# Casting the keys' and channel weights' high parts on GpSimd instead of ScalarE

## Chip, cores and metric

The kernel runs on one core of one Trainium2 chip. The metric is the device time of one execution in microseconds (us); three runs of the kernel before gave 1030.22, 1030.34 and 1031.10 us, with a median of 1030.34 us.

## The reference, cut to what matters

Three parts follow one another. Everything is fp32 at the interface; there are 4 batches, 8 heads, 576 tokens, head dimension 64.

```python
# 1. attention with a threshold, per batch and head
scores = q @ k.T / 8
scores = where(scores >= max(scores) - tau, scores, -1e9)
attn = softmax(scores)
x = (attn @ v)                       # heads side by side: [4, 576, 512]
# 2. token mixing of rank 32, then a channel layer
u = x + (x.T @ U @ V).T
x = u + relu(u @ w_ch1) @ w_ch2      # 512 -> 2048 -> 512
# 3. a mixture of 8 experts, one expert per token
out[token] = p[e] * relu(x[token] @ w1[e]) @ w2[e]
```

## The kernel before, in words

**Numbers in two parts.** TensorE (PE) multiplies in a shortened fp32 form here (`F32R` in the code). To keep the precision, many operands are split: a high part, which is the number rounded to that form, and a low part, which is the number less its high part. A product is then built from two or three matmuls. The splitting costs one copy (the high part) and one subtraction (the low part) for each tile.

**Attention.** The 8 heads of a batch are handled as 4 pairs, so there are 16 pairs `i`, 0 to 15, with batch `b = i // 4`. `load_pair` (L261) loads one pair. It walks over `cuts`: for pairs 1 to 15 these are two cuts of the keys (576 and 640 columns, `kq` = 1) and then two of the queries (608 columns each). Each cut is one DMA from the queue on SyncE (SP) into a raw tile `x` (three such buffers, L281), then the split: for keys the high part `kh` by ScalarE (ACT, L289) and the low part `kl` by the engine called `eng` (L290), which is GpSimd (POOL) for pairs 1 to 7 and VectorE (DVE) for pair 0 and for batches 2 and 3 (L271). For queries ACT makes the high part (L292) and DVE the low one (L294). The tiles `kh` and `kl` have two buffers each, so those of a pair come free when the scores of the pair two before it are done.

Per pair there are five groups of rows, and the scores of a pair come in nine tiles of 576 columns. A tile goes through: scores on PE (L313, L315), row maximum on DVE (L348), exponential on ACT (L359), a limit and then mask with row sum on DVE (L352, L363). There are two PSUM buffers for scores, so the scores of a tile wait for the mask of the tile two before it. The back half transposes the result on PE (L416, L422), copies it to SBUF on ACT (L417, L423, L424), multiplies by the values (L435 to L439), and then a chain of small steps (`chain`, L447) does the token mixing.

**Stages.** Batch 0 has attention alone (`attention_alone`, L553): while its tiles run, ACT and DVE also convert the channel weights from their 64-bit form (`narrow`, L198; a cast on ACT at L212, a join on DVE at L219), which SP writes to DRAM (`wdram`). `turn_over` (L580) puts dummy matmuls into PE's gaps. Then batches 1 to 3 run their attention interleaved with the channel layer of the batch before (`channel`, L725). The channel layer takes its weights from `wdram` with `load_w` (L664): one tile for each of the two layers per block `f` (16 blocks), each split into `hi` and `lo`. In batch 0 the high part is made by ACT for `f` 0 and 1 and by POOL after that (L677 to L680); the low part is by POOL in batch 0 (L676, L681). After the last attention come the last channel layer, the routing, and the experts.

**What sets the order.** The instructions are written in program order with data dependences; a planner places them on the engines' queues by its own estimates of their times, earliest first where inputs and buffers are ready. Each engine then works through its queue in order. Only in `attention_alone` is the order of one engine, POOL, kept as written (L855). So moving an instruction to another engine can also move others on all queues.

The choice of engine for the high part in `load_w`:

```python
eng = dve if b and (b < B - 1 or f < 8) else pool
if b == 0 and f > 1:
    pool.tensor_copy(hi, x)
else:
    act.activation(hi, x, AF.Copy)
```

Of the kernel before, what the change touches and what calls it, by code (L numbers as in the profile page):

```python
# [14 lines left out]
AF = mybir.ActivationFunctionType  # L15
# [88 lines left out]
def attention_channel_moe(ctx, tc, qk, vv, tau, umat, vrep, wch, wgl, wexp, consts, out):  # L104
    nc = tc.nc
    pe, dve, act, pool, sp = nc.tensor, nc.vector, nc.scalar, nc.gpsimd, nc.sync
# [146 lines left out]
    def scalars():  # L253

        sp.dma_start(out=t8[:, 0:1], in_=tau)

        dve.tensor_scalar(out=t8[:, 1:2], in0=t8[:, 0:1], scalar1=NEGTAU, scalar2=0.125, op0=ALU.is_ge, op1=ALU.mult)
        dve.tensor_scalar(out=t8[:, 2:3], in0=t8[:, 1:2], scalar1=0.0, scalar2=BIG, op0=ALU.is_equal, op1=ALU.mult)
        dve.tensor_scalar(out=t8[:, 0:1], in0=t8[:, 0:1], scalar1=0.0, scalar2=t8[:, 2:3], op0=ALU.max, op1=ALU.add)

    def load_pair(b, hp, later=None):  # L261

        i = b * NPAIR + hp
        v = ap.tile([128, VW], F32, tag="v", name=f"v{i}")
        qs = ap.tile([128, QKW], F32R, tag="qs", name=f"qs{i}")
        kh = ap.tile([128, QKW], F32R, tag="kh", name=f"kh{i}")
        kl = ap.tile([128, QKW], F32R, tag="kl", name=f"kl{i}")

        cuts = ((0, 0, 128), (1, 0, S), (0, 704, 832), (1, S, QKW), (0, 128, 704), (0, 832, QKW)) if i == 0 else (
            (1, 0, S), (1, S, QKW), (0, 0, 608), (0, 608, QKW))  # L270
        eng = dve if i == 0 or b > 1 else pool  # L271
        def steps():
            for n, (kq, c0, c1) in enumerate(cuts):
                c = slice(c0, c1)
                nm = f"raw{i}_{n}"
                if (i, n) == (0, 1):
                    x = mlp.tile([128, S], F32, tag="yr", name=nm, bufs=2)
                elif i == 0 and c1 - c0 == 128:
                    x = mlp.tile([128, 512], F32, tag="wr", name=nm, bufs=WR)
                else:  # L280
                    x = ap.tile([128, 640], F32, tag="raw", name=nm, bufs=3)  # L281
                x = x[:, :c1 - c0]
                sp.dma_start(out=x, in_=qk[i][:, kq, c])
                if (i, n) == (0, 0):
                    scalars()
                if (i, n) == (0, 3):
                    sp.dma_start(out=cst, in_=consts)
                if kq:
                    act.activation(kh[:, c], x, AF.Copy)  # L289
                    eng.tensor_tensor(out=kl[:, c], in0=x, in1=kh[:, c].bitcast(F32), op=ALU.subtract)  # L290
                else:
                    act.activation(qs[:, c], x, AF.Copy, scale=t8[:, 1:2])  # L292
                    lo, hi, xl = qs[64:128, c], qs[64:128, c].bitcast(F32), x[64:128]
                    dve.scalar_tensor_tensor(out=lo, in0=xl, scalar=t8[64:128, 1:2], in1=hi,  # L294
                                             op0=ALU.mult, op1=ALU.subtract)
                yield
            sp.dma_start(out=v, in_=vv[i])

        if later is None:
            for _ in steps():  # L300
                pass
        else:
            later.append(steps())
        return qs, kh, kl, v
# [359 lines left out]
    def load_w(b, f):  # L664
        nm = f"{b}_{f}"
        if f >= NF or nm in W:
            return
        while DONE[0] < f:
            next(conv, None)
        r = []  # L670
        for i, bufs in ((0, W0), (1, W1)):
            x = mlp.tile([128, 512], F32, tag="wr", name=f"wr{nm}_{i}", bufs=WR)
            sp.dma_start(out=x, in_=wdram[f * 128:f * 128 + 128, i * 512:i * 512 + 512])
            hi = mlp.tile([128, 512], F32R, tag=f"w{i}h", name=f"w{i}h{nm}", bufs=bufs)
            lo = mlp.tile([128, 512], F32R, tag=f"w{i}l", name=f"w{i}l{nm}", bufs=bufs)
            eng = dve if b and (b < B - 1 or f < 8) else pool  # L676
            if b == 0 and f > 1:  # L677
                pool.tensor_copy(hi, x)
            else:
                act.activation(hi, x, AF.Copy)  # L680
            x = eng.tensor_tensor(out=lo, in0=x, in1=hi.bitcast(F32), op=ALU.subtract)  # L681
            if i == 0:
                LAST[:] = [x.ins]
            r.append((hi, lo))
        W[nm] = r
# [39 lines left out]
    def channel(p):  # L725
        hs = {}
        load_w(p, 0)
        load_w(p, 1)
        for f in range(NF):
            yield from mlp_l1(p, f, hs)  # L730
            if f % 4 == 0 and f:
                yield from mlp_l2(p, f - 4, hs)
            load_w(p, f + 2)
        HS[p] = hs
# [640 lines left out]
```

## Time and profile before

| What | Value |
|---|---|
| median of three runs | 1030.34 us |
| the profiled execution, its own time | 1029.61 us |
| its span, first to last instruction | 1027.8 us |
| mean granted TensorE clock | 0.996 of full speed |
| PE busy, share of the span | 995.2 us, 97% |
| DVE busy | 719.3 us, 70% |
| ACT busy | 611.8 us, 60% |
| POOL busy | 152.2 us, 15% |

The profiled execution's own time has 1.8 us that lie around its span. A row of the trace gives an engine and an operation with the source line, "out<-in" names, shapes, a count, busy time and a mean; behind a bar or in brackets stands how long the engine sat idle just before it and what ended that. Busy shares are averages over stages that have different limits, so the stretches of the span are read one by one.

### The profile page before, as it was taken

What the parts mean: (1) busy time and instruction counts of PE and PEld (TensorE: products, weight loads), DVE (VectorE), ACT (ScalarE), POOL (GpSimd) and SP (SyncE); (2) the same over time, 40 slices, a digit from 0 to 9 for tenths busy, and PEclk for the clock granted to TensorE, in tenths of its full rate; (3) what the DMA queues carried; (4) which work ended last, traced back from release to release, by engine and by line L of the source; (5) the groups of instructions that cost most, each with busy time, mean ns of one, the idle gap of its engine ahead of it and who ended that gap; (6) DMA issues with size and microseconds to landing.
All of it is one profiled execution on the core that took longest, in us unless ns stands there. A gap on an engine that the chain in (4) does not pass through costs nothing. (4 is left out here: it accounts for less than half of the span.)

```text
span 1027.8 us, 17859 instructions
## 1 busy us (share of the span) xinstructions
PE 995.2 (97%) x6352; PEld 836.2 (81%) x6352; DVE 719.3 (70%) x1761; ACT 611.8 (60%) x1242; POOL 152.2 (15%) x143
## 2 busy tenths in 40 slices
PE   7898999989999999999999999999999999999996
PEld 4666677768787787788889898999998998889984
DVE  7998697776778877877676664683369755566673
ACT  6888777776677777776565653422354444455562
POOL 1332245342000000000000000013400321120100
PEclk9999999999999999999999999999999999999998
DMA  6655577864323322423121110453055555566550
GB/s 213 220 153 162 160 257 245 273 209 140 116 92 94 125 72 83 127 90 94 55 68 42 42 43 31 139 207 122 25 192 180 177 202 185 174 192 198 196 184 16
DMA packets 58241, 143.72 MB, mean 140 GB/s; under 512 B 7389, under 2 KB 8157, under 8 KB 58144
## 3 DMA queue, kind: packets, MB, share of 16 engines
q1 hardware_dynamic: 54784, 132.27, 40.0%
q0 software_dynamic: 3360, 10.23, 3.1%
q8 instruction: 52, 0.85, 0.3%
q14 instruction: 45, 0.37, 0.1%
HBM read 124.65 MB, written 18.61 MB: 139 GB/s over the span
## 5 line engine op out<-in xcount | busy, mean ns | idle before, releaser
L1125 ACT ACTIVATE eh<-ew 128x512 fp32r<-128x512 f32 x160 | 94.2, 628 | 68.1 <-PE el L1241 47.7
L1126 DVE TENSOR_TENSOR el<-ew,eh 128x512 fp32r<-128x512 f32 x160 | 106.7, 692 | 37.7 <-ACT eh L1125 36.2
L702 PE MATMUL l<-uh,w0h 128*128 128x256 f32 (+2 forms) x352 | 127.0, 361 | 0.3 <-ACT yT L508 0.3
L363 DVE SCALAR_TENSOR_TENSOR p<-s,st,p 128x576 f32<-128x576 f32 x144 | 114.1, 814 | 15.8 <-ACT p L359 12.4
L359 ACT ACTIVATE p<-s,st 128x576 f32<-128x576 f32 x144 | 103.7, 738 | 33.1 <-DVE st L348 31.6
L703 PE MATMUL l<-ul,w0h 128*128 128x256 f32 (+2 forms) x352 | 122.6, 348 | 0.0
L704 PE MATMUL l<-uh,w0l 128*128 128x256 f32 (+2 forms) x352 | 122.3, 348 | 0.0
L348 DVE TENSOR_REDUCE st<-s 128x1 f32<-128x576 f32 x144 | 105.1, 749 | 18.0 <-PE s L315 17.4
L717 PE MATMUL l<-hh,w1h 128*128 128x512 f32 (+3 forms) x320 | 115.2, 360 | 0.0
L719 PE MATMUL l<-hh,w1l 128*128 128x512 f32 (+3 forms) x320 | 112.8, 353 | 0.0
L718 PE MATMUL l<-hl,w1h 128*128 128x512 f32 (+3 forms) x320 | 112.2, 351 | 0.0
L417 ACT ACTIVATE ptt<-tp 128x512 f32<-128x512 f32 (+1 forms) x192 | 88.4, 490 | 30.1 <-PE tp L416 30.0
L313 PE MATMUL s<-kh,qs 128*128 128x288 f32 x320 | 95.5, 318 | 5.6 <-DVE p L363 3.6
L681 POOL TENSOR_TENSOR w1l<-wr,w1h 128x512 fp32r<-128x512 f32 x24 | 31.7, 1333 | 457.5 <-DVE rha L984 426.6
L416 PE MATMUL tp<-cst,p 128*128 128x128 f32 x576 | 90.8, 276 | 5.2 <-ACT ptt L417 5.0
L722 DVE TENSOR_TENSOR yT<-l,yT 128x448 f32<-128x448 f32 (+2 forms) x96 | 50.0, 521 | 57.9 <-PE l L719 57.5
L315 PE MATMUL s<-kl,qs 128*128 128x288 f32 x320 | 88.5, 296 | 0.0
L373 ACT ACTIVATE p<-p,rv 128x576 f32<-128x576 f32 x108 | 78.6, 771 | 15.3 <-DVE rv L380 15.0
L416 PEld LDWEIGHTS tp<-cst,p 128*128 128x128 f32 x576 | 67.8, 140 | 20.6 <-ACT ptt L417 11.4
L313 PEld LDWEIGHTS s<-kh,qs 128*128 128x128 f32 x320 | 60.3, 188 | 15.6 <-DVE p L363 6.4
L435 PE MATMUL po<-ptt,v 128*64 128x256 f32 (+1 forms) x256 | 69.8, 413 | 2.4 <-ACT ptt L424 1.5
L706 DVE SCALAR_TENSOR_TENSOR hl<-l,hh 128x512 fp32r<-128x512 f32 (+2 forms) x80 | 46.3, 578 | 36.7 <-ACT hh L705 36.4
(604 smaller groups left out, 2468.6 us busy)
## 6 DMA issues: line engine op xcount, KB each, us to landing
ew<-in_wexp_dram SPq DMA_DIRECT2D x80, 512.0 KB, 4.6
wr<-wdram SPq DMA_DIRECT2D x128, 256.0 KB, 3.1
cr<-in_wch_dram SPq DMA_DIRECT2D x32, 512.0 KB, 5.2
raw<-in_qk_dram SPq DMA_DIRECT2D x30, 304.0 KB, 3.2
wdram<-w SPq DMA_DIRECT2D x32, 256.0 KB, 3.0
v<-in_vv_dram SPq DMA_DIRECT2D x16, 352.0 KB, 3.9
raw<-in_qk_dram SPq DMA_DIRECT2D x16, 320.0 KB, 3.8
raw<-in_qk_dram SPq DMA_DIRECT2D x17, 288.0 KB, 3.0
```

The lines of the kernel that those rows point to most:

```text
L313: pe.matmul(s["t"][:, h, :288], lhsT=qs[:, qc:qc + 128], rhs=kh[:, k0:k0 + 288], start=(j == 0), stop=False)
L348: dve.tensor_reduce(out=self.st[:, 0, h:h + 1], in_=self.t[h], axis=AX.XY, op=ALU.max, negate=True)
L359: act.activation(self.halves(h), self.t[h], AF.Exp, bias=self.st[:, 0, h:h + 1])
L363: dve.scalar_tensor_tensor(out=p, in0=self.t[h], scalar=self.st[:, 1, h:h + 1], in1=p, op0=ALU.is_ge, op1=ALU.mult, accum_out=self.rvs[:, ...
L416: pe.transpose(tp[:, c - c0], src[:, c * 128:c * 128 + 128], ident)
L702: pe.matmul(pm, lhsT=w1h[:, wk], rhs=uh[k], start=(k == 0), stop=False)
L703: pe.matmul(pm, lhsT=w1h[:, wk], rhs=ul[k], start=False, stop=False)
L704: pe.matmul(pm, lhsT=w1l[:, wk], rhs=uh[k], start=False, stop=(k == 3))
L717: pe.matmul(pm, lhsT=w2h[:, wd], rhs=xh, start=(f == f0), stop=False)
L718: pe.matmul(pm, lhsT=w2h[:, wd], rhs=xl, start=False, stop=False)
L719: pe.matmul(pm, lhsT=w2l[:, wd], rhs=xh, start=False, stop=(f == f0 + 3))
L1126: dve.tensor_tensor(out=lo, in0=x, in1=hi.bitcast(F32), op=ALU.subtract)
```

## The change

It does two things. In `load_pair`, where the low parts of the keys are already POOL's (pairs 1 to 7), POOL also makes the high parts with a copy. In `load_w`, POOL makes the high parts of all blocks of batch 0, those of `f` 0 and 1 too.

```diff
@@ load_pair
                 if kq:
-                    act.activation(kh[:, c], x, AF.Copy)
+                    if eng is pool:
+                        pool.tensor_copy(kh[:, c], x)
+                    else:
+                        act.activation(kh[:, c], x, AF.Copy)
                     eng.tensor_tensor(out=kl[:, c], in0=x, in1=kh[:, c].bitcast(F32), op=ALU.subtract)
@@ load_w
             eng = dve if b and (b < B - 1 or f < 8) else pool
-            if b == 0 and f > 1:
+            if b == 0:
                 pool.tensor_copy(hi, x)
             else:
                 act.activation(hi, x, AF.Copy)
```

## Rows read from the trace of the kernel before

**Rows 1.** Busy time by stretch: start:end, length, PE, PEld, DVE, ACT, POOL (instructions).

```profile
8.00:103.00 95.00, 81.91 (x568) 59.27 (x567) 87.85 (x207) 76.73 (x159) 25.72 (x20) 1.00 0.61 188
103.00:240.00 137.00, 130.15 (x787) 99.59 (x786) 107.26 (x225) 101.93 (x198) 51.78 (x50) 1.00 0.72 231
240.00:622.00 382.00, 381.29 (x2444) 314.23 (x2443) 271.84 (x678) 256.57 (x520) 7.54 (x8) 1.00 0.26 81
...
750.00:1000.00 250.00, 249.19 (x1500) 223.31 (x1500) 166.50 (x373) 119.23 (x238) 36.59 (x35) 1.00 0.56 186
```

**Rows 2.** Waits of DVE, 8 to 103 us: total us, times, longest.

```profile
DVE st L348 <- PE s L315: 4.6, 7, 1.2
DVE p L363 <- ACT p L359: 1.2, 2, 0.9
DVE qs L294 <- ACT qs L292: 0.4, 1, 0.4
```

**Rows 3.** Waits of PE, 8 to 103 us.

```profile
PE tp L416 <- ACT ptt L417: 5.0, 7, 1.3
PE s L313 <- DVE p L363: 2.8, 4, 2.2
PE s L313 <- DVE st L352: 1.7, 2, 1.5
PE po L435 <- ACT ptt L423: 0.6, 2, 0.3
PE idle L585 <- ACT ptt L417: 0.6, 1, 0.6
```

**Rows 4.** ACT's key copies (L289) by form and waits of ACT, 8 to 103 us.

```profile
L289 ACT ACTIVATE kh<-raw 128x640 fp32r<-128x640 f32 x5 | 3.7, 738 | 0.6 <-DMA raw<-in_qk_dram 0.6
L289 ACT ACTIVATE kh<-raw 128x576 fp32r<-128x576 f32 x5 | 3.4, 681 | 1.4 <-issue 0.8 <-POOL w1l L681 0.6
...
ACT qs L292 <- DMA raw<-in_qk_dram: 2.3, 4, 0.8
```

**Rows 5.** ACT's high parts of weight blocks 0 and 1, from L680, 0 to 103 us.

```profile
L680 ACT ACTIVATE w0h<-wr x2: 632/632/632, 46.3 to 60.4; 128x512 fp32r<-128x512 f32 x2
L680 ACT ACTIVATE w1h<-wr x2: 621/629/637, 50.2 to 68.4; 128x512 fp32r<-128x512 f32 x2
```

**Rows 6.** POOL's work by form, 8 to 103 us.

```profile
L290 POOL TENSOR_TENSOR kl<-raw,kh 128x640 fp32r<-128x640 f32 x5 | 8.3, 1651 | 0.0
L290 POOL TENSOR_TENSOR kl<-raw,kh 128x576 fp32r<-128x576 f32 x5 | 7.5, 1495 | 18.6 <-ACT kh L289 18.5
...
L678 POOL CAST w1h<-wr 128x512 fp32r<-128x512 f32 x1 | 0.6, 612 | 15.9 <-DMA wr<-wdram 15.9
```

**Rows 7.** DVE by form, 8 to 103 us, and the line L219 over the span.

```profile
L294 DVE SCALAR_TENSOR_TENSOR qs<-raw,t,qs 64x608 fp32r<-64x608 f32 x10 | 9.3, 926 | 0.7 <-ACT qs L292 0.4
L219 DVE SCALAR_TENSOR_TENSOR w<-cr,top 128x512 int32<-128x512 int32 x7 | 7.6, 1085 | 0.0
...
L379 DVE TENSOR_SCALAR rv<-rv 128x4 f32<-128x4 f32 x8 | 3.5, 444 | 0.1
...
L219 DVE SCALAR_TENSOR_TENSOR w<-cr,top x32: 670/690/1721, 32.0 to 231.8; 128x512 int32<-128x512 int32 x32
```

**Rows 8.** Order of time, one meeting of DVE and POOL: start, us.

```profile
155.40 1.13 DVE L219 SCALAR_TENSOR_TENSOR w<-cr,top 128x512 int32<-128x512 int32 x1
...
155.38 0.61 POOL L678 CAST w1h<-wr 128x512 fp32r<-128x512 f32 x1 [3.18 <-PE l L718]
```

**Rows 9.** Order of time: pair 2's keys, its first scores; then L313 by stretch.

```profile
31.41 0.69 POOL L237 TENSOR_TENSOR vst<-wv,vst 32x64 fp32r<-32x64 f32 x2 [0.93 <-DVE vst L235]
32.18 3.35 POOL L290 TENSOR_TENSOR kl<-raw,kh 128x576 fp32r<-128x576 f32 x2
...
51.54 0.30 PE L313 MATMUL s<-kh,qs 128*128 128x288 f32 x1
...
0.00:51.53 51.53, 12.91 (x40) 7.68 (x41) 1.00 0.68 216
```

**Rows 10.** Waits of SP's queue, 8 to 103 us; first use of the channel weights.

```profile
SPq L283 <- POOL kl L290: 23.1, 8, 9.4
...
L702 PE MATMUL l<-uh,w0h x352: 277/365/631, 113.3 to 745.2; 128*128 128x512 f32 x64, 128*128 128x256 f32 x48, 128*128 128x448 f32 x32, 128*128 128x320 f32 x32
```

**Rows 11.** Waits of PE, 103 to 240 us.

```profile
PE tx L461 <- ACT yT L442: 2.0, 2, 1.2
PE po L435 <- ACT ptt L424: 1.5, 2, 0.8
```

## The prediction

> **What bounds the kernel now.** I read the busy time by stretch first [rows 1]. From 240 us on PE is busy for 381.29 of 382 us and for 249.19 of 250 us; PE is the bound there and nothing in the change touches that part. In 103 to 240 us (attention of batch 1 beside the channel layer of batch 0) PE still works 130.15 of 137 us. Only 8 to 103 us is different: PE 81.91 of 95 us, dummy matmuls included, DVE 87.85, ACT 76.73, POOL 25.72. So in the first attention DVE is the engine that is nearly full (92%), ACT follows with 81%, and PE waits for both. A shorter first stretch moves everything behind it forward by the same amount, since PE then works without a gap.
>
> Next, what DVE waits for in that stretch [rows 2]: 4.6 us for scores from PE, 1.2 us for an exponential from ACT, 0.4 us for a query cut from ACT. These 6.2 us are nearly all of its 7.15 idle us, and they are the most that the stretch can lose unless DVE gets less work, which the change does not give it. Why scores are late is seen in the waits of PE [rows 3]: the listed waits on ACT come to 6.2 us, those on DVE to 4.5 us. PE takes its queue in order, so scores stand behind a transpose that waits for ACT to empty its PSUM tile. That is the way in which a full ACT reaches DVE.
>
> **Part 1, ACT gets less work.** In 8 to 103 us there are ten key copies (pairs 1 to 5): 5 x 0.738 + 5 x 0.681 = 7.1 us by the two forms [rows 4]. The four weight copies of blocks 0 and 1 are 2 x 0.632 + 2 x 0.629 = 2.5 us [rows 5]. ACT thus loses 9.6 of 76.7 us, and goes from 81% to 71%. It also loses about 2 us in which it stood still in front of a key copy whose DMA or buffer was not ready [rows 4], with exponentials queued behind. What this is worth on the path: at least nothing, at most the 6.2 us of DVE's waits. I take the 1.6 us that ACT itself ended (1.2 + 0.4) in full, and 1.0 us of the 4.6 us that came through PE: ACT has more than half of PE's waits, some 2.7 of the 4.6, and I count a little over a third of that because ACT's load falls by an eighth only and some of the waits are PE's own matmuls at the end of a pair. Gain 2.6 us.
>
> **Part 2, POOL gets more work.** A copy of 128x512 takes POOL 0.612 us [rows 6]. By the number of columns I estimate 0.69 us for 576 and 0.765 us for 640. Fourteen copies in the stretch are 5 x 0.69 + 5 x 0.765 + 4 x 0.612 = 9.7 us; POOL goes from 25.7 to 35.4 of 95 us. POOL itself is not the bound.
>
> But POOL's instructions hold up some of DVE's. A join on DVE that starts 0.02 us after a POOL copy of 0.61 us takes 1.13 us [rows 8]; its usual duration is 0.69 us [rows 7]. So a plain copy does it too, at 0.44 us in this case. What it costs in sum is read from the means of the three kinds that are stretched [rows 7]: joins 7 x (1.085 - 0.69) = 2.8 us; the query cuts 10 x (0.926 - 0.85) = 0.8 us; the small 128x4 additions at 8 x (0.444 - 0.16) = 2.3 us, where 0.85 and 0.16 us are my estimates of what such an instruction takes undisturbed, from the shortest part of each group. That is 5.9 us of DVE's time against 25.7 us of POOL's: 0.23 us per us of POOL work. For 9.7 us this gives 2.2 us. The other end is half of that, 1.1 us: what a collision costs is what is left of POOL's instruction, so the cost per instruction grows with the square of its length, and the copies are half as long as POOL's subtractions (0.7 against 1.3 to 1.65 us). I take the middle, 1.6 us, since the copies stand directly in front of the subtractions and do not come at free moments.
>
> The Trainium skill (SBUF — State Buffer, "Who interferes with whom") states that VectorE with two SBUF inputs and GpSimd reading SBUF share an exclusive port, and that the second to start blocks fully until the first is done. By that alone that join [rows 8] would lose the 0.59 us left of the copy instead of 0.44 us, and the 1.6 us would become about 2.1 us. The row decides, and the sum stays with 1.6 us.
>
> **Part 3, the order of things inside a pair.** POOL now does copy, subtraction, copy, subtraction on its own queue, where ACT's copies ran ahead of it. For pair 2, whose subtractions stand behind POOL's `vst` work until 32.1 us [rows 9], the first subtraction ends 0.7 us later. SP's load of the last query cut waits for that raw buffer [rows 10], and ACT's query copy waits for the load (2.3 us, four times [rows 4]), with exponentials behind it. Bounds: 0.7 us earlier for a pair where POOL was idle and ACT busy, 0.7 us later where POOL is busy; for five pairs -3.5 to +3.5 us. I take nothing: both kinds occur, and the finished keys have much room (pair 2 is done at 35.5 us and first used at 51.54 us: a pair has 20 matmuls of line L313, and 40 lie before that [rows 9]). If the planner puts the query copy too early on ACT, this cover is gone, at up to 0.7 us each.
>
> The four weight copies cost nothing beyond the port: they are made by 70 us and used from 113.3 us on [rows 10]. POOL waits for their DMA as it does for the ones after them, and only low parts that need the same data stand behind.
>
> **Part 4, 103 to 240 us.** The four copies of pairs 6 and 7 leave ACT (2 x 0.738 + 2 x 0.681 = 2.8 us of 101.9) and put 2.9 us on POOL. PE is the bound, with 6.85 us idle; the two longest waits on ACT are 2.0 and 1.5 us [rows 11]. Gain between nothing and 0.5 us, taken as nothing. The port takes 0.7 us from DVE at the same rate, hidden because DVE is busy for 78% only; without that cover it costs 0.7 us.
>
> **Sum.** -2.6 + 1.6 = -1.0 us on the profiled execution of 1029.61 us: 1028.6 us. That execution lies 0.73 us below the median of 1030.34 us, so in terms of the median: **1029.3 us**. About 0.2% (2.1 us) is what a measurement of this kernel can tell from no change; the forecast is inside that.
>
> There is one cost without a row: the planner places all queues anew. The bound for it is PE's idle time that an order can win or lose, 13.1 us in the first stretch and 6.85 us in the second; a fifth of it, 4 us either way, is my estimate.
>
> **Rivals.**
> - *ACT was the hidden bound of the first stretch* (chance 0.34). PE's longest waits are for ACT [rows 3]. If the lighter ACT clears DVE's waits almost wholly and the port costs the low end, it is -6.2 + 1.1 = -5.1 us at most, 1025.2 us; with half of the 6.2 us plus 1 us from the second stretch, -3.0 us, 1027.3 us. Against it: DVE has 92% of the stretch without any help, and its waits on ACT are 1.2 and 0.4 us.
> - *The port makes it slower* (chance 0.23). Where copy and subtraction of one cut follow each other without a pause, POOL is in the way for about 2.2 us instead of 1.5 us, and a join or a query cut that arrives can lose all of it. At one and a half times the rate, 0.34 us per us, 9.7 us cost 3.3 us; if ACT's relief is worth nothing because DVE is the bound, this is +3.3 us: 1033.6 us. It decides from the point where the holding costs 2.1 us more than the relief gives. For it: DVE is the fullest engine and works 20 us of the stretch in instructions that can be held. Against it: at today's rate the cost is at most 2.2 us. The Trainium skill (Perfetto Trace Analysis, "Optimizing Scalar/DVE Operations") warns that moving work between these two engines might not help because of the shared port; no run so far shows it for the move from ACT.
> - *Nothing moves* (part of the 0.43 for "same"). The copies lay in ACT's own idle time, 18 us of the stretch, so relief and port are both small: 1030.3 us.
>
> **How the numbers follow.** The forecast and "nothing moves" lie within 2.1 us of 1030.34 us: 0.43. Faster 0.34, slower 0.23. The range goes from 1025.0 us (first rival at its end) to 1034.5 us (second rival with some of part 3); the forecast's own range is 1028.2 to 1032.4 us.
>
> **What would show it.** In 8 to 103 us ACT should be near 67 us busy, POOL near 35 us, and the joins' mean a little above 1.085 us. DVE's waits on ACT should be nearly gone, the first pair of batch 1 should begin 1 us earlier. POOL copies should measure 0.69 and 0.765 us. Wrong would be: DVE's stretched instructions growing by over 3 us, new waits of ACT for query DMAs, or a first stretch that is shorter with the time given back in 103 to 240 us.

## The result and the profile after

The changed kernel is slower. Eleven runs have a median of 1037.58 us (1033.59 to 1040.54); eleven runs of the kernel before on the same chip have 1030.35 us (1029.36 to 1032.84). The ratio is 1.0066, with a 95% interval of 1.0055 to 1.0077. The forecast was 1029.3 us, and the result lies outside its range (1025.0 to 1034.5 us). The profiled execution after took 1037.8 us, with a span of 1036.0 us; each is 8.2 us more than in the profiled execution before.

Line numbers of the changed kernel are 3 higher from L293 on (POOL's key copy is L290, ACT's is L292); in the kernels of the experiments they are shifted by up to 5 lines. First the busy time by stretch; columns as in [rows 1], where PEld is the weight load of PE and the last three numbers are the granted clock, the DMA share and GB/s.

```profile
8.00:103.00 95.00, 80.74 (x535) 56.86 (x535) 83.65 (x199) 66.44 (x136) 33.76 (x33) 0.96 0.56 176
103.00:240.00 137.00, 127.21 (x752) 95.46 (x751) 107.70 (x217) 98.97 (x191) 58.83 (x56) 1.00 0.68 222
240.00:622.00 382.00, 381.32 (x2455) 314.95 (x2454) 276.62 (x687) 257.10 (x519) 7.56 (x8) 1.00 0.27 86
```

Against [rows 1]: ACT fell by 10.3 us and POOL rose by 8.0 us in the first stretch, as meant. But DVE, which sets that stretch, fell too, by 4.2 us: it was not relieved, it stood still. PE's idle time in the second stretch rose from 6.85 to 9.79 us. From 240 us on PE is as full as before. One row says how the loss is spread: the first and the last use of the channel weights.

```profile
L705 PE MATMUL l<-uh,w0h x352: 276/366/632, 119.2 to 753.9; 128*128 128x512 f32 x64, 128*128 128x256 f32 x48, 128*128 128x448 f32 x32, 128*128 128x320 f32 x32
```

Before it was 113.3 to 745.2 us [rows 10]: 5.9 us are lost before the channel layer of batch 0 begins, 2.8 us after that. The seventeenth row maximum on DVE, at 46.22 us before and 52.39 us after, is already 6.2 us late, so nearly all of the first stretch's loss is made by then.

What DVE, PE and ACT waited for in 8 to 103 us (total, times, longest), from the waits of the changed kernel:

```profile
DVE st L351 <- PE s L318: 7.5, 14, 1.3
PE s L316 <- DVE p L366: 6.0, 5, 2.2
ACT qs L295 <- DMA raw<-in_qk_dram: 2.6, 3, 1.3
PE idle L588 <- ACT ptt L420: 2.2, 1, 2.2
ACT p L362 <- DVE st L351: 10.7, 12, 2.4
DVE qs L297 <- ACT qs L295: 0.7, 1, 0.7
```

and the last but one of these in the kernel before:

```profile
ACT p L359 <- DVE st L348: 3.7, 7, 1.4
```

DVE waits 7.5 us for scores instead of 4.6 us, 14 times instead of 7 [rows 2]. PE's longest wait of before, for ACT to empty a transpose (5.0 us [rows 3]), is down to 0.3 us, but PE now waits 6.0 us for masks of DVE instead of 2.8 us, and ACT 10.7 us for row maxima instead of 3.7 us: ACT is lighter, and stands longer. ACT's waits for raw query cuts are hardly more than before, 2.6 us in 3 waits against 2.3 us in 4. None of these rows names POOL: a reader who only looks for POOL among the releasers finds nothing. The three kinds of DVE instruction that POOL can hold up are seen by form:

```profile
L297 DVE SCALAR_TENSOR_TENSOR qs<-raw,t,qs 64x608 fp32r<-64x608 f32 x9 | 9.1, 1016 | 0.3
L219 DVE SCALAR_TENSOR_TENSOR w<-cr,top 128x512 int32<-128x512 int32 x7 | 7.2, 1025 | 0.0
L382 DVE TENSOR_SCALAR rv<-rv 128x4 f32<-128x4 f32 x8 | 3.0, 370 | 0.0
```

Against [rows 7] the query cuts grew by 9 x 0.09 = 0.8 us, the joins shrank by 7 x 0.06 = 0.4 us and the small additions by 8 x 0.07 = 0.6 us. In sum DVE is held no longer than before. POOL's copies of keys take 7.4 us in all, where 7.3 us were worked out:

```profile
L290 POOL CAST kh<-raw 128x576 fp32r<-128x576 f32 x5 | 3.8, 763 | 14.9 <-DMA raw<-in_qk_dram 10.7 <-PE s L316 4.1
L290 POOL CAST kh<-raw 128x640 fp32r<-128x640 f32 x5 | 3.6, 718 | 0.0
```

Two things are new near the start. The first is the fourth load of pair 1, its last query cut. In order of time, SP's queue, first the kernel before and then the changed one:

```profile
17.01 0.33 SPq L283 DMA_DIRECT2D raw<-in_qk_dram  x1
```

```profile
20.47 6.68 SPq L283 DMA_DIRECT2D raw<-in_qk_dram  x4
```

It leaves 3.5 us later. In the kernel before the three raw buffers go round: the load takes the buffer of pair 1's first key cut, which POOL frees. In the plan of the changed kernel it takes the buffer of the cut just before it, which DVE frees.

The second is PE's clock, by stretches of 2 us (the third number from the end is the granted clock):

```profile
14.00:16.00 2.00, 0.61 (x4) 0.61 (x5) 1.76 (x6) 1.10 (x2) 1.92 (x3) 0.98 1.00 377
16.00:18.00 2.00, 2.00 (x11) 1.90 (x9) 1.10 (x5) 0.86 (x2) 1.33 (x1) 0.50 0.08 25
18.00:20.00 2.00, 0.75 (x4) 0.45 (x3) 1.97 (x5) 1.83 (x4) 0.00 (x0) 0.50 0.00 0
20.00:22.00 2.00, 1.78 (x7) 1.03 (x8) 1.97 (x5) 0.13 (x1) 0.00 (x0) 0.50 0.28 46
```

From 16 us on PE has half its clock (1.2 instead of 2.4 GHz) until it rises again between 22 and 24 us. It fell behind a stretch in which it worked 0.61 of 2 us. In the kernel before the clock stood at 1.00 from the start to the tail. The last digits of the third of these rows show no DMA at all: SP was standing in front of that load.

### The profile page after: what moved, and what is told of

Its sections match the earlier page's. It is cut to its first block, busy times and chain, and to the rows that moved or that the text cites. A ratio compares the mean times of both kernels' runs of the same rounds, so it can differ in the third digit from the quotient of the medians.

```text
span 1036.0 us, 17857 instructions
## 1 busy us (share of the span) xinstructions
PE 999.5 (96%) x6351; PEld 836.8 (81%) x6352; DVE 723.3 (70%) x1761; ACT 603.6 (58%) x1224; POOL 168.3 (16%) x161
## 5 line engine op out<-in xcount | busy, mean ns | idle before, releaser
L705 PEld LDWEIGHTS l<-uh,w0h 128*128 128x128 f32 x352 | 66.5, 189 | 6.8 <-DVE rsm L800 0.7
```

Of the source, the lines that this page charges most:

```text
L705: pe.matmul(pm, lhsT=w1h[:, wk], rhs=uh[k], start=(k == 0), stop=False)
```

## The experiments

Each was timed against the kernel before on its own chip. The kernel before came out at 1030.35 to 1031.12 us in five comparisons and at 1034.05 us in one, so ratios are what to compare.

### One part at a time

The edits, from the kernel before: `pairs_only` has the `load_pair` part and `weights_only` the `load_w` part; `pair1_only` moves pair 1's two key copies alone; `all_but_pair1` is the whole change without those two.

```diff
 # pair1_only
-                    act.activation(kh[:, c], x, AF.Copy)
+                    if i == 1:
+                        pool.tensor_copy(kh[:, c], x)
+                    else:
+                        act.activation(kh[:, c], x, AF.Copy)
 # all_but_pair1: the change, with this condition
+                    if eng is pool and i > 1:
```

> Edit: only the key copies of pairs 1 to 7 move to GpSimd; the weight copies stay as before. Theory A (the raw buffers: with pair 1's copies on GpSimd the fourth cut of pair 1 gets a raw buffer that a VectorE instruction sets free, SyncE's queue stands until about 20.5 us, the first attention falls behind and PE's clock falls with it): 1035 to 1039 us, nearly all of the loss, SyncE's fourth load of pair 1 at about 20 us. Theory B (the shared port: each copy on GpSimd holds VectorE): 14 of 18 copies remain, so 1035 to 1036 us, but with VectorE's joins and query cuts longer by some 4 us in sum.

> Edit: only the four weight copies of blocks 0 and 1 move to GpSimd. Theory A: the loads up to 40 us are planned as before, so 1029 to 1031.5 us. Theory B: 4 of 18 copies, 1031.5 to 1032.5 us.

> Edit: only the two key copies of pair 1 move to GpSimd; the others and the weights stay as before. Theory A: the same wrong buffer, so most of the loss from two copies: 1033 to 1038 us, the fourth load at about 20 us. Theory B: 2 of 18 copies, 1030.5 to 1031.5 us.

> Edit: the whole change, but pair 1's key copies stay on ScalarE. Theory A: the loads up to 24 us are planned as before, the clock stays up; 1027 to 1031.5 us, perhaps faster than before since ScalarE has less work. Theory B: 16 of 18 copies, 1036 to 1037 us.

| run | median, us | ratio to the kernel before [95% interval] |
|---|---|---|
| pairs_only | 1039.57 | 1.0080 [1.0064, 1.0095] |
| weights_only | 1029.95 | 0.9993 [0.9984, 1.0002] |
| pair1_only | 1033.92 | 1.0034 [1.0020, 1.0049] |
| all_but_pair1 | 1036.73 | 1.0061 [1.0048, 1.0074] |

The weight copies cost nothing that can be told from zero; the whole loss is in the key copies. Pair 1 alone costs about half, but leaving pair 1 out saves next to nothing. So the one late load of pair 1 can't be the only cause, and theory A fell in its pure form. Theory B, the port, met its range only with `all_but_pair1` and missed the other three. In all four the planner had placed all queues anew, so what a copy does and what a new order does were still mixed.

### Holding the order still

The next kernels take the planner's order out. The changed kernel and the kernel before issue the same instructions one for one, but for the engine of 18 copies. A list of the order in which the planner had put one kernel's instructions is therefore valid for the other, and ties without a wait between neighbours of a queue force it:

```python
def keep_order(tc):                  # called behind the last attention
    traced = {i.name: i for i in tc.nc.cur_bb.bb.instructions}
    for names in ORDER.values():     # PE, DVE, ACT, SP: instruction numbers, as planned
        last = None
        for x in names.split():
            i = traced.get("I-" + x)
            if i is None or (last is not None and i.engine != last.engine):
                continue             # a copy that is on POOL now
            if last is not None:
                tc.add_manual_dep(i, last.name, mybir.DependencyInfo(
                    mybir.DependencyClass.NoSync, mybir.DependencyReason.DATA), reason="order")
            last = i
```

`change_in_old_order` is the change with the list of the kernel before, `old_engines_in_new_order` the kernel before with the list of the changed one. `port_alone` leaves ACT's copies where they were and adds copies on POOL (`EXTRA` keeps their names, so that the numbers of the list still fit):

```diff
+                    if eng is pool:
+                        EXTRA.append(pool.tensor_copy(kl[:, c], x).ins.name)
                     eng.tensor_tensor(out=kl[:, c], in0=x, in1=kh[:, c].bitcast(F32), op=ALU.subtract)
...
+            if b == 0 and f < 2:
+                EXTRA.append(pool.tensor_copy(lo, x).ins.name)
```

`change_with_warm_pe` leaves the planner free and adds dummy matmuls:

```diff
-            turn_over(int((0.8 - spent) / 0.2), i)
+            turn_over(int((0.8 - spent) / 0.2) + {2: 2, 3: 5, 4: 5, 5: 3, 6: 4, 7: 3, 8: 3}.get(i, 0), i)
```

> The whole change, but PE, DVE, ACT and SP keep the order of the kernel before instruction for instruction (edges without a wait between neighbours of a queue, up to the end of the last attention); only the 18 moved copies stand on POOL. Theory 'order' (the loss comes from the order in which the planner places all queues once the copies leave ACT): the loss is gone, 1027 to 1031 us, and what is left is the prediction's sum of relief and port, -1.0 us. Theory 'engines' (POOL's copies hold up DVE or come too late): still 1036 to 1039 us. Theory 'clock' (PE's clock falls by itself after its early gaps, whatever the order): a fall at 14 to 22 us again and 1033 to 1037 us.

> The kernel before, all copies on ACT, but PE, DVE, ACT and SP are held to the order of the changed kernel. Theory 'order': slow like the changed kernel, 1034 to 1040 us, although no copy has moved. Theory 'engines': like the kernel before, 1029 to 1032 us.

> The kernel before in its own order, with 18 copies more on POOL: each key cut of pairs 1 to 7 and each weight tile of blocks 0 and 1 is also copied by POOL into the tile of its low part, which the subtraction then overwrites. ACT keeps its copies, so this is POOL's new work without ACT's relief. The prediction's term for the port is +1.6 us (bounds 1.1 to 3.3 us). Theory 'order' with the trace of the changed kernel (the stretched instructions of DVE grew by 0.4 us only): 0 to +1.5 us, 1029.5 to 1032 us. Theory 'engines': +4 us or more, over 1034 us.

> The whole change with 25 dummy matmuls more in the first nine steps of the first attention, to fill PE's early gaps. The planner places everything anew here too. Theory 'clock': no stretch at 0.50 before 40 us, and 1030 to 1034 us. Theory 'order': the clock holds, but DVE still waits for scores in 20 to 100 us, and the time stays at 1033 to 1038 us. Theory 'engines': 1036 to 1039 us.

| run | median, us | ratio |
|---|---|---|
| change_in_old_order | 1038.33 | 1.0071 [1.0053, 1.0089] |
| old_engines_in_new_order | 1038.56 | 1.0067 [1.0048, 1.0085] |
| port_alone | 1037.51 | 1.0075 [1.0052, 1.0097] |
| change_with_warm_pe | 1035.99 | 1.0045 [1.0029, 1.0061] |

No theory expected both of the first two to be slow. The new order costs 7 us with all copies on ACT; the copies on POOL cost 7 us in the old order. They don't add up: the change with both costs 7.2 us. Why they don't is not shown. ACT's waits for raw query cuts, which matter below, are not what makes the new order slow: in `old_engines_in_new_order` they are shorter in 8 to 103 us than in the kernel before (2.3 us, 4 times [rows 4]):

```profile
ACT qs L292 <- DMA raw<-in_qk_dram: 2.0, 3, 1.1
```

With the dummies the ratio is 1.0045 instead of 1.0066, some 2 us, and the intervals touch. The clock held in the first 38 us of that run and fell at 38 to 42 us and near 192 us instead. The planner also placed everything anew here. So the clock is at most a part of the loss, as far as this run can tell.

`port_alone` can be read instruction by instruction, since PE, DVE, ACT and SP have the same work in the same order as before. Until 20 us it runs beside the kernel before within 0.6 us; then ACT stands still (order of time, ACT, in brackets the idle time before; first the kernel before, then `port_alone`):

```profile
19.89 0.80 ACT L292 ACTIVATE qs<-raw,t 128x608 fp32r<-128x608 f32 x1 [0.37 <-DMA raw<-in_qk_dram]
...
20.99 0.75 ACT L359 ACTIVATE p<-s,st 128x576 f32<-128x576 f32 x1
```

```profile
18.76 0.76 ACT L420 ACTIVATE ptt<-tp 128x512 f32<-128x512 f32 x2
22.98 0.80 ACT L295 ACTIVATE qs<-raw,t 128x608 fp32r<-128x608 f32 x1 [3.46 <-DMA raw<-in_qk_dram]
...
23.92 0.72 ACT L362 ACTIVATE p<-s,st 128x576 f32<-128x576 f32 x1
```

ACT's next instruction is pair 1's query copy, and its data is not there. An exponential is queued behind it and starts at 23.92 us, where the kernel before started it at 20.99 us. The Trainium skill (TensorE: Matmul & The Clock Gate, "Architectural detail: the array is 16× 32×32, not 1× 128×128") states that ACT and DVE take their queues strictly in order; this row is what that does here, 3.46 us for one late load. The load itself went out at 20.00 us, because in this plan too it had been given the buffer of the cut before it.

### The raw buffers

Now the buffers are named by hand as well. `RAW` says for every cut which of the three it takes. In the kernel before they simply go round (`abca` for pair 1, `bcab` for pair 2); in the plans with more work on POOL pair 1 reads `abcc`, and then they go round again.

```diff
-                    x = ap.tile([128, 640], F32, tag="raw", name=nm, bufs=3)
+                    x = ap.tile([128, 640], F32, tag="raw" + RAW[i][n], name=nm, bufs=1)
```

`buffer_alone` is the kernel before, in its order, with the buffers of the changed plan. The other three have the buffers of the kernel before: the change in the old order, the added copies in the old order, and the change with the planner free.

> The kernel before, with its engines and its order. Only the raw buffers are named by hand, as the planner dealt them out for the changed kernel: pair 1's last query cut takes the buffer of the cut just before it and not the one of pair 1's first key cut; from there on the three go round as before. Theory 'buffer' (with slower keys on POOL the planner expects that buffer first, and on the chip it comes free 3 us later): the load starts near 20 us and not at 17 us, the seventh score tile is late by 2.5 to 3 us, and the time is 1034 to 1039 us although no copy has moved. Theory 'engines' (POOL's copies themselves cost the time): 1029 to 1032 us.

> The whole change in the order of the kernel before on PE, DVE, ACT and SP, with the raw buffers named by hand so that they go round as in the kernel before. Nothing differs from the kernel before but the engine of the 18 copies. Theory 'buffer': the loss is gone, and what is left is relief and port, predicted as -2.6 + 1.6 = -1.0 us: 1027 to 1031.5 us. Theory 'engines': 1035 to 1039 us.

> As port_alone (18 copies more on POOL, ACT keeps its own), with the raw buffers going round as in the kernel before. Theory 'buffer': what is left is the price of the port and of later low parts alone, 0 to +2 us: 1030.5 to 1033 us. Theory 'engines': 1035 us or more, as without the buffers.

> The whole change with the planner's own new order, and only the raw buffers named by hand so that they go round as in the kernel before. Theory 'buffer' alone: 1028 to 1032 us. Theory 'order' (the new places on all queues cost something of their own, as the kernel before lost 7 us when it was held to the new order): 1033 to 1038 us.

| run | median, us | ratio |
|---|---|---|
| buffer_alone | 1037.15 | 1.0033 [1.0016, 1.0050] |
| change_old_order_old_buffers | 1040.91 | 1.0069 [1.0046, 1.0092] |
| port_alone_old_buffers | 1039.86 | 1.0066 [1.0044, 1.0088] |
| change_old_buffers | 1047.67 | 1.0128 [1.0100, 1.0155] |

The one buffer costs some 3 us with no copy moved. (Its 1037.15 us lie in the range that theory 'buffer' gave, but on this chip the kernel before took 1034.05 us; on one where it takes 1030.35 us the ratio makes 1033.8 us, just below that range.) But giving the buffer back does not help, and that was a miss for the theory. With the planner free it even made the worst kernel of the study, which no theory explains. The rows of `port_alone_old_buffers` show why the old rotation is not enough. Pair 1's load now leaves at 17.22 us. For pair 2 the same thing happens through POOL itself; in order of time SP and ACT of the kernel before, then POOL, SP and ACT of this run:

```profile
34.01 0.33 SPq L283 DMA_DIRECT2D raw<-in_qk_dram  x1
...
37.12 0.80 ACT L292 ACTIVATE qs<-raw,t 128x608 fp32r<-128x608 f32 x1 [0.83 <-DMA raw<-in_qk_dram]
37.83 0.72 ACT L359 ACTIVATE p<-s,st 128x576 f32<-128x576 f32 x1
```

```profile
34.22 1.08 POOL L293 CAST kl<-raw 128x576 fp32r<-128x576 f32 x1
35.38 1.42 POOL L294 TENSOR_TENSOR kl<-raw,kh 128x576 fp32r<-128x576 f32 x1
...
36.83 0.33 SPq L285 DMA_DIRECT2D raw<-in_qk_dram  x1
...
40.10 0.80 ACT L296 ACTIVATE qs<-raw,t 128x608 fp32r<-128x608 f32 x1 [1.92 <-DMA raw<-in_qk_dram]
40.81 0.72 ACT L363 ACTIVATE p<-s,st 128x576 f32<-128x576 f32 x1
```

POOL comes to pair 2's keys only behind its `vst` work. Where the kernel before starts the subtraction at once [rows 9], a copy of 1.08 us stands in front of it. The raw buffer comes free at 36.8 us instead of 34.0 us: POOL's first instruction for this pair starts 2.0 us later than in the kernel before, a delay that is older than the copy, and the other 0.8 us are the copy's. SP's load goes out then, and ACT's query copy waits 1.92 us instead of 0.83 us, with the exponential behind it. In the old order the change itself shows this chain at its full size: in `change_in_old_order` pair 1's query copy waits 3.27 us and pair 2's 2.86 us, where the kernel before has 0.37 and 0.83 us (in that run, too, pair 1's load has the other buffer).

```profile
24.13 0.80 ACT L295 ACTIVATE qs<-raw,t 128x608 fp32r<-128x608 f32 x1 [3.27 <-DMA raw<-in_qk_dram]
...
42.62 0.80 ACT L295 ACTIVATE qs<-raw,t 128x608 fp32r<-128x608 f32 x1 [2.86 <-DMA raw<-in_qk_dram]
```

All four queues pass the delay on in order: POOL holds a buffer, SP holds the load, ACT holds the exponentials, DVE holds the masks.

The older delay of 2.0 us falls together with the clock. Between the reductions of the fourth and the eighth score tile the same instructions take 8.78 us in the kernel before and 10.67 us here:

```profile
16.02 0.76 DVE L348 TENSOR_REDUCE st<-s 128x1 f32<-128x576 f32 x1
...
24.80 0.76 DVE L348 TENSOR_REDUCE st<-s 128x1 f32<-128x576 f32 x1
```

```profile
16.17 0.76 DVE L352 TENSOR_REDUCE st<-s 128x1 f32<-128x576 f32 x1
...
26.84 0.76 DVE L352 TENSOR_REDUCE st<-s 128x1 f32<-128x576 f32 x1 [0.23 <-PE s L319]
```

DVE's own instructions grew by 0.1 us in between, and the busy times by stretch of this run show PE's clock at half:

```profile
18.00:20.00 2.00, 0.84 (x3) 0.87 (x4) 1.97 (x5) 1.71 (x4) 1.48 (x1) 0.50 0.69 188
20.00:22.00 2.00, 1.78 (x6) 0.94 (x7) 1.94 (x5) 1.39 (x3) 0.00 (x0) 0.50 0.70 201
```

So up to the eighth tile this fall cost some 1.8 us, as far as one profiled run can tell. Whether it is still lost at the end is another question; the last section of the experiments has a run with the same fall that is not slower than the kernel before.

### Cutting the chain

The last query cut of a pair gets a tile that POOL never holds, one of the channel layer's `hh` buffers that are idle during the first attention. It covers pairs 1 to 5. The cuts become 640 and 576 columns, to fit it.

```diff
-            (1, 0, S), (1, S, QKW), (0, 0, 608), (0, 608, QKW))
+            (1, 0, S), (1, S, QKW), (0, 0, 640), (0, 640, QKW))
...
+                elif 0 < i <= 5 and n == 3:
+                    x = mlp.tile([128, S], F32, tag="hh", name=nm, bufs=5)
```

The first two runs have it in the order of the kernel before, with and without the change; the other two with the planner free.

> The whole change in the order of the kernel before, and the last query cut of pairs 1 to 5 is loaded into a tile of its own (a buffer of the channel layer that is idle then; the two query cuts are 640 and 576 columns). SP's load of it no longer waits for POOL. Theory 'chain' (POOL holds the raw buffer longer, the load is late, ACT's query copy blocks the exponentials): most of the loss is gone, 1028 to 1033 us, and ACT's waits for query cuts in 8 to 60 us are under 1 us. Theory 'port or late keys': still 4 us or more above the same kernel without the change. Theory 'clock': falls in the first 50 us in both kernels.

> The same with the copies on ACT as in the kernel before: the control. Theory 'chain': the loads were 0.8 us late at most in the kernel before, so this gains 0 to 1.5 us: 1028.5 to 1031 us. The difference to the run with the change is then relief and port alone, between -2 and +1 us. Theory 'port or late keys': the run with the change is slower by 4 us or more.

> The whole change and the own query tile, with the planner free. Theory 'chain': 1027 to 1033 us. Theory 'order' (the new places on the queues cost something of their own): 1033 us or more.

> Only the weight part of the change, and the own query tile, with the planner free. If cutting the chain is worth something in itself: 1026 to 1029.5 us, faster than both kernels. If the planner's new order costs what it cost in the other kernels: 1032 to 1036 us.

| run | median, us | ratio |
|---|---|---|
| change_own_query_tile_old_order | 1030.51 | 0.9998 [0.9984, 1.0013] |
| before_own_query_tile_old_order | 1030.39 | 0.9993 [0.9983, 1.0003] |
| change_own_query_tile | 1038.09 | 1.0076 [1.0059, 1.0093] |
| weights_own_query_tile | 1031.93 | 1.0007 [0.9993, 1.0022] |

This settles what the copies cost in the old order. With the chain cut and the order held, the whole change costs nothing that can be told from zero: 1030.51 against 1030.39 us. Without the cut it cost 7 us in the same order. ACT's waits for raw query cuts in 8 to 103 us, first `change_in_old_order`, then this run:

```profile
ACT qs L295 <- DMA raw<-in_qk_dram: 8.1, 5, 3.3
```

```profile
ACT qs L297 <- DMA raw<-in_qk_dram: 0.5, 1, 0.5
```

then the busy time in the first stretch of the control (`before_own_query_tile_old_order`), the busy times of the changed run, and its first and last use of the weights, at 112.3 and 745.7 us:

```profile
8.00:103.00 95.00, 82.56 (x573) 59.63 (x575) 87.62 (x209) 77.47 (x165) 25.71 (x20) 1.00 0.62 190
```

```profile
8.00:103.00 95.00, 82.39 (x575) 59.88 (x576) 86.60 (x210) 70.32 (x151) 36.38 (x34) 1.00 0.62 194
103.00:240.00 137.00, 128.65 (x780) 98.68 (x778) 107.22 (x222) 98.93 (x188) 55.91 (x54) 1.00 0.71 226
```

```profile
L707 PE MATMUL l<-uh,w0h x352: 277/366/632, 112.3 to 745.7; 128*128 128x512 f32 x64, 128*128 128x256 f32 x48, 128*128 128x448 f32 x32, 128*128 128x320 f32 x32
```

POOL is busy for 36.38 us in the first stretch, more than in the changed kernel, and it does no harm; ACT works 70.32 us instead of 77.47 us, and it does no good that is seen. The clock stands at 1.00 in both rows, so this execution had no fall. Not all of its twelve are like that: the four slowest, 1032.65 to 1033.98 us, have a mean clock of 0.990 to 0.994. The Trainium skill (Perfetto Trace Analysis, "Optimization Strategy") states that a gap that repeats on the engine that should be saturated can mean that there is not enough memory for the next tile to be allocated. The trace agrees as to the remedy, though the gaps here are on ACT, which is not the fullest engine: a place of its own for one cut of a pair took the waits from 8.1 to 0.5 us.

The third run shows the second cause, the new order, alone. With the chain cut and the planner free the change is as slow as ever. It issues the same instructions as the first run, on the same chip, and differs in where the planner put them: 1038.09 against 1030.51 us. Its waits of ACT and DVE, and those of DVE in `old_engines_in_new_order` (8 to 103 us):

```profile
ACT qs L297 <- DMA raw<-in_qk_dram: 0.7, 1, 0.7
DVE st L353 <- PE s L320: 8.8, 13, 1.7
DVE p L368 <- ACT p L364: 0.8, 2, 0.6
```

```profile
DVE st L348 <- PE s L315: 7.1, 14, 1.5
DVE qs L294 <- ACT qs L292: 3.4, 4, 1.3
DVE p L363 <- ACT p L359: 2.6, 4, 1.3
```

In both, scores reach DVE late 13 or 14 times, as in the changed kernel. The count alone is no sign of a bad order, though: the fastest version, below, has 11 such waits with 6.1 us in its profile. Which place in the order does it was not found. That a new order need not be bad is seen in `weights_only` and, nearly, in the fourth run, whose 1031.93 us lie between the two ranges expected of it.

What this says of the changed kernel itself: its order alone is enough for its whole loss (1.0067 with no copy moved, against 1.0066), and its own rows show no more waiting for raw query cuts than before. In the old order the chain alone is enough as well. Whether the chain still costs anything in the new order is not shown: no run has the changed kernel's exact order with the chain cut.

### Putting the harmless parts together

```diff
-            if b == 0 and f > 1:
+            if b == 0:
```

with the own query tile and the old order.

> The two parts that did no harm put together: only the weight copies of blocks 0 and 1 on POOL, the own query tile for pairs 1 to 5, and PE, DVE, ACT and SP in the order of the kernel before. Each alone came out 0.7 us below the kernel before (ratio 0.9993). Theory 'chain' and 'order' together: nothing is lost, 1028.5 to 1030.5 us, and if the two gains add up the ratio is 0.9986. If the planner's order was not what made the same edits 1.2 us slower when it was free: 1031 to 1033 us.

It came out at 1029.61 us against 1031.12 us, 1.5 us less by the medians, with a ratio of 0.9981 [0.9970, 0.9993]. The interval ends just below 1. One such interval among the 17 of these experiments is weak evidence for a gain of 0.2%, so this version is at least not slower than the kernel before, and perhaps a little faster. Each part alone could not be told from no change.

Its profiled execution, at 1029.04 us, also bears on the clock. It has a fall at the same place as the changed kernel:

```profile
18.00:20.00 2.00, 1.00 (x4) 0.98 (x4) 1.94 (x6) 2.00 (x5) 0.52 (x1) 0.50 0.78 175
```

Its eighth score reduction is at 26.73 us, 1.9 us later than before, and yet the channel weights are first used at 113.5 us and last at 745.0 us, as in the kernel before (113.3 and 745.2 us [rows 10]):

```profile
L704 PE MATMUL l<-uh,w0h x352: 277/366/631, 113.5 to 745.0; 128*128 128x512 f32 x64, 128*128 128x256 f32 x48, 128*128 128x448 f32 x32, 128*128 128x320 f32 x32
```

So one early fall is not by itself a loss at the end.

## Why the prediction was wrong

Two steps failed, and for the changed kernel as it was timed it is the first of them. *The cost without a row*, the new places on all queues, was left out of the sum and bounded at 4 us either way; it was worth 7 us the wrong way. *Part 3*, the order of things inside a pair, was taken at nothing; in the old order it was worth 7 us as well. Either alone is as large as the whole loss.

**What bounds the kernel** held. The loss is made where the first attention and the stretch to 240 us have their idle time, and everything behind it moved as a whole, by 8.7 us at the last use of the weights.

**Part 1, ACT's relief**, was near in its size on ACT: 9.6 us less were predicted and 10.3 us measured, of which some is work that no longer fell into the stretch. Between the two runs with the own tile, whose counts of ACT instructions differ by just the 14 copies of the stretch (165 and 151), it is 77.47 - 70.32 = 7.2 us. The gain of 2.6 us on the path did not show. With the chain cut and the order held, relief and port together come to 1030.51 - 1030.39 = 0.1 us, where -1.0 us was predicted; the two intervals overlap widely, so neither zero nor -1.0 us is excluded.

**Part 2, the port**, was put at +1.6 us. The three stretched kinds changed by -0.2 us in sum in the changed kernel, and between the two runs with the own tile from 20.2 to 18.7 us, with the query cuts of 576 and 640 columns counted together. So no price of the port is seen in either pair of traces, although POOL worked 8 to 11 us more. The rival that gave the port the loss had the right sign and the wrong mechanism: at 1033.6 us its price was half of what came, and the holding that it built on did not grow.

**Part 3, the order of things inside a pair**, named the chain, POOL to the raw buffer to SP's load to ACT's query copy, and then took it at nothing, with bounds of 3.5 us either way. Three things were wrong with that. Its price per pair was set at 0.7 us, the length of POOL's copy, but with the copies moved in the old order ACT waited 2.9 us more than before in front of pair 1's query copy and 2.0 us more in front of pair 2's; part of the first came from the planner, which had given that load another buffer. The late side was set off against an early side: pair 1's load can leave earlier, at 15.28 us in `change_old_order_old_buffers` and at 13.09 us in `before_own_query_tile_old_order`, but the latter with its ratio of 0.9993 shows no gain from it. And the cover named there, the room that the finished keys have, covers the scores of the next pair and not the exponentials that stand behind the query copy; the text says so in its last sentence and gives it no weight.

**Part 4, 103 to 240 us**, was taken at nothing. PE's idle time there rose by 2.9 us, and 2.8 us were lost behind the first use of the weights. No run tells the causes of this part apart.

**The cost without a row**, the planner's new places, was named but not counted. The kernel before, put into the new order with no copy moved, lost 7 us (1.0067), and the change with its chain cut takes 1038.09 us in a new order and 1030.51 us in the old one. The bound was a fifth of PE's idle time; the new order made idle time of its own. Which move in it does the harm stays open.

**The clock** had no term. Falls go with a good part of the loss: the two of the changed kernel's eleven runs with the highest mean clock (0.998 and 0.997) took 1033.6 and 1034.7 us, so in them 3 to 4 us of the loss of 7 us remain. But the run with a fall and no loss shows that a fall need not cost anything at the end.

**What would show it** was right in part. ACT came out near 67 us and POOL near 35 us, as said; the joins got shorter and not longer. "New waits of ACT for query DMAs" is on the list of what would be wrong, and it is what the change brings in the old order (8.1 us against 2.3 us). In the changed kernel itself, at 2.6 us, it did not come, and the new order was not on the list.

## What to carry to other kernels

When a step moves to a slower engine, follow the buffer that it reads, not only what it writes: who loads into that buffer next, on which queue that load stands, and what waits in order behind the reader of that load. Price that chain from its late side alone, since an earlier load brought nothing here. And where a planner places the queues, time the edit once in the old order before judging it, because a new order alone cost 7 us here, as much as the copies did in the old one.

## What was not expected of the hardware

PE stood idle for 2.18 us at 13 us in both profiled runs, before and after (in order of time, PE, the kernel before and the changed one):

```profile
15.19 0.40 PE L313 MATMUL s<-kh,qs 128*128 128x288 f32 x1 [2.18 <-DVE p L363]
```

```profile
15.39 0.40 PE L316 MATMUL s<-kh,qs 128*128 128x288 f32 x1 [2.18 <-DVE p L366]
```

Behind the second the clock fell to half (1.2 GHz) and behind the first it did not. The changed kernel had paused once more before that, for 0.65 us at 11.3 us; in `all_but_pair1`, where PE did not, the clock fell between 14 and 16 us all the same. So the same pause can be followed by a fall or not. The runs of the kernel before differ too. On the chip where its median was 1034.05 us, four of its five runs with a mean granted clock of 0.996 or more took 1030.4 to 1030.7 us and the fifth 1034.05 us, and its seven with 0.993 or less 1033.8 to 1036.6 us. On the chip where its median was 1030.92 us, six runs with 0.993 took only 1030.85 to 1032.12 us. So the mean clock does not give the time by itself, and what decides is not shown by any run here.
